# Two attention blocks on one core: fewer bound products, Strassen sums left in PSUM, a different cost for ScalarE in the list scheduler

## The chip, the cores and the metric

The kernel runs on one core of one Trainium2 chip. The core has a matmul engine (TensorE, PE in the profile, with PEld for its weight loads), VectorE (DVE), ScalarE (ACT), GpSimd (POOL), and SyncE (SP), which here only issues DMA transfers. On-chip memory is SBUF; matmul results land in PSUM, which the kernel hands out as eight banks of 128 x 512 float32, and which GpSimd does not touch in this kernel. The metric is the device time of one execution in microseconds. The inputs are float32; for its large products the kernel splits each operand into two float16 halves and multiplies three of the four pairs of halves.

## The reference

Two independent attention blocks over 2048 tokens and 1024 features, 32 heads of 32; their outputs stand side by side.

```python
# block A: causal softmax attention in 4 segments of 512, with a compressive memory
for s in range(4):
    logits = einsum("bhqd,bhkd->bhqk", qs, ks) * scale + mask
    a_dot = softmax(logits) @ vs
    a_mem = (phi(qs) @ M) / (phi(qs) @ z + 1e-6)          # phi(t) = t + 1 if t > 0 else exp(t)
    outs.append(g * a_mem + (1 - g) * a_dot)
    M, z = M + phi(ks).T @ vs, z + sum(phi(ks))
a = concat(outs) @ A_wo
# block B: linear attention with a learned feature map
q, k, v = split(B_x @ B_wqkv)
phi_q = concat(softmax(q @ w_phi), softmax(-(q @ w_phi)))   # phi_k likewise, from k
kv, z = phi_k.T @ v, sum(phi_k)
b = ((phi_q @ kv) / (phi_q @ z + 1e-6)) @ B_wo
out = concat(a, b, axis=-1)
```

## The kernel before

The program runs five stages, one after the other with some overlap. The times are those of the windows in the profile.

1. **Attention of block A** (about 0 to 870 us). There are 32 units: a unit `u` is one segment of 512 tokens and one group of four heads. `produce(u)` projects queries, keys and values of a unit (L369 matmuls into `proj` banks), and `attend(u)` does row maxima (L801, L807), scores (L902), exponentials (L906), the split of the probabilities into halves (L908 on ScalarE, L909 on VectorE), masks (L915 on GpSimd) and the product with the values (L938). Segments 0 and 1 are done for all eight head groups first, then segments 2 and 3. Meanwhile the weights of block B are folded, combined and split in the background (`fold`, `weights_v`, `prepare`).
2. **Values of block B for three of the eight token pairs** (about 870 to 960 us), with `strassen`.
3. **Keys** (about 960 to 1290 us): for each of eight token pairs a Strassen product for keys and, for five pairs, one for values; `expo` makes the two softmaxes of the keys, and L1350 accumulates the key-value sums.
4. **Queries** (about 1290 to 1600 us): Strassen products for queries, `expo` again, the products with the sums, and the output projection of block B (L369 into `misc`).
5. **Output projection of block A** (about 1600 to 1766 us), a Strassen product in place (L1590).

Before a projection is made, its size must be bounded, because the float16 halves need a scale. The bound of a group is the product of the largest column sum of its weights and the largest entry of the segment. `bounds(k, segs)` (queries and keys) and `bounds_v(k, segs)` (values) build it with a tiny matmul that sums over the partitions (L687: 128 x 2, L708: 128 x 1) and a few tiny operations on VectorE and GpSimd. `k` runs over 16 (group, half) pairs for queries and keys and over 8 for values; each call handles two segments with one matmul each.

The weights of a head group are loaded by `load_wg`, scaled and split into float16 halves by `halves`. Its default (`sub=DVE`) is one ScalarE copy with a scale (L396) and one VectorE subtraction (L398); for the first two groups the caller passes `POOL`, which scales and subtracts on GpSimd (L390, L393).

`strassen` makes four 128 x 512 output blocks from seven products of twelve matmuls each. Three PSUM banks X, Y, Z hold the products. Three partial sums are copied from PSUM to SBUF by ScalarE (`keep`, L583), and VectorE adds a product from PSUM to the copy in place (`add`, L587). The callback `out` then reads three of the four blocks from SBUF (tile `cs`, or `pk` in stage 2) and the fourth from the PSUM bank. In stages 3 and 4 `out` is `expo`: two reductions (L1192), two subtractions (L1194, L1196), four exponentials on ScalarE (L1199), a sum (L1202), for keys a multiplication of the 128 x 32 sums by a constant (L1204), and a reciprocal (L1205). For keys GpSimd then multiplies the exponentials by the reciprocals (L1308). For values `out` is `vout` (L1230 on ScalarE, L1232 on VectorE).

The order on each engine is not the order of the Python code. Every operation is recorded with its engine, a cost in microseconds, its reads and writes and a priority; `Graph.run` then places them one by one like a list scheduler: the engine that can start first takes, among its ready operations, the one with the lowest priority number. The costs and the latencies between engines (`Graph.LAT`) are constants in the code. An operation marked `port` on VectorE is not placed while the plan has GpSimd busy, nor the other way round. PSUM banks are given out in the same loop, with a limit for each kind (`MOST`). A DMA issue is an operation on SP; `lanes` are two dummy tiles: loads that write the same lane are placed one behind the other. The real program gets only the resulting order and semaphores for true dependences, so a wrong cost makes no error, only a worse order.

Of the kernel before, what the change touches and what calls it, by code (L numbers as in the profile page):

```python
# [78 lines left out]
class Graph:  # L79
# [35 lines left out]
    def op(self, eng, dur, fn, r=(), w=(), prio=0, lat=0.0, short=False, port=False, need=(), kb=256):  # L115
        o = Op()
        o.short, o.port = short, port or eng == "POOL"
        o.eng, o.dur, o.fn, o.prio, o.lat, o.kb = eng, dur, fn, (prio, len(self.ops)), lat, kb
# [137 lines left out]
def tile_kernel(ctx: ExitStack, tc: tile.TileContext, ax, aw, awv, awo, beta, bx, bwqk, bwv, bphi, bwo, out):  # L256
# [52 lines left out]
    nc.vector.memset(big, 0.0)  # L309
    wsc = const.tile([128, 3, 2, 2], F32, name="wsc")  # L310
# [75 lines left out]
    def halves(hi, lo, src, sc, n, prio, port=True, sub=DVE):  # L386

        (hb, hk, hv), (lb, lk, lv), (sb, sv), (cb, ck, cv) = hi, lo, (src[:-1] if len(src) > 2 else src[0], src[-1]), sc
        if sub == POOL:
# [167 lines left out]
    def xkept(p, slots, prio):  # L557
# [5 lines left out]
        for f in XORDER:  # L563
            b, i = where[f]
            op(SP, 0.6, lambda b=b, i=i, f=f: nc.sync.dma_start(b()[:, i], xf_d[p, :, f]),
               r=[(xfb, (p, f))], w=[(b, (f, a)) for a in range(2)], prio=prio, lat=1.0, kb=256)
        return view_

    def strassen(x, w, prio, kinds, tag, out):
# [16 lines left out]
        def add(t, ps):  # L586
            op(DVE, 0.62, lambda: nc.vector.tensor_tensor(t(), t(), ps(), op=OP.add), r=[ps], w=[t], prio=prio)  # L587
# [4 lines left out]
        add(p1, Y)  # L592
        out(0, 0, p1)
# [5 lines left out]
        add(p5, X)  # L599
        out(1, 1, p5)  # L600
        mult(Z, 5)
        add(u2, Z)
        out(0, 1, u2)
# [21 lines left out]
    pstb, wmb, topb = (G.fixed(t) for t in (pst, wm, tops))  # L625
# [53 lines left out]
    def bounds(k, segs, prio):  # L679


        bd = bds.get(k) or bds.setdefault(k, G.buf("a", [128, 5, 2, 2], F32, "bd", 4))
        s0, n, kk = segs[0], len(segs), k % NG
        v, w = slice(s0 % 2, s0 % 2 + n), [(bd, x % 2) for x in segs]
        ps = bank("misc", [128, 2, 2], "bounds")
        for x in segs:
            op(PE, 0.14, lambda x=x: nc.tensor.matmul(  # L687
                ps()[:, x % 2], xam[:, x:x + 1].to_broadcast([128, 128]), wgb[:, kk], start=True, stop=True),
               r=[(xams, x), (wgbs, (kk, 0)), (wgbs, (kk, 1))], w=[ps], prio=prio, need=[bd])
        op(DVE, 0.1, lambda: nc.vector.tensor_scalar(bd()[:, 3, v], ps()[:, v], 2.0 ** -12, 1e-30, op0=OP.mult, op1=OP.max),  # L690
           r=[ps], w=w, prio=prio)
        op(DVE, 0.12, lambda: nc.vector.reciprocal(bd()[:, 2, v], bd()[:, 3, v]), w=w, prio=prio)
# [778 lines left out]
    for c in range(NT):  # L1471
        P = Q0 + c
        if c % 2 == 0:
# [6 lines left out]
            if c + 2 < NT:  # L1480
                x = xkept(c // 2 + 1, XB if c == 0 else XS, P)
# [180 lines left out]
```

## Time and profile before

| what | us |
|---|---|
| median of 3 runs | 1764.49 (1764.32 to 1765.12) |
| the profiled execution's own time | 1767.9 |
| its span, first to last instruction | 1766.2 |
| PE / DVE / ACT / POOL busy | 1714.1 / 1430.7 / 1147.8 / 978.2 |

The profiled execution lies 3.4 us above the median, and 1.7 us of its time are outside the span. Busy times are unions of the instructions' intervals. A matmul's record runs until its result has drained, so consecutive records overlap, and small waits inside a stream of matmuls do not show as idle time. Groups are listed as "line engine operation out<-in, count | busy us, mean ns of one | idle time before them and what ended it". Tile names are given without their buffer numbers.

### The profile page before, as it was taken

How to read it: one execution, taken by the hardware profiler on the slowest of the kernel's cores; microseconds unless marked ns; L12 is line 12 of the kernel's file. 1: busy time of each engine (PE TensorE's matmuls, PEld its weight loads, DVE VectorE, ACT ScalarE, POOL GpSimd, SP SyncE). 2: the span in 40 equal slices, each digit the busy share in tenths (PEclk: the TensorE clock that was granted, in tenths of full speed). 3: DMA queues.
4: the chain of work that ended last, by engine and by line, in shares of the span. 5: the costliest groups of instructions: out<-in, count | busy, mean ns of one | idle time of the engine just before them, and what ended most of it. 6: DMA issues, size and time to landing. Idle time of an engine off the chain costs nothing.

```text
span 1766.2 us, 39229 instructions
## 1 busy us (share of the span) xinstructions
PE 1714.1 (97%) x14722; PEld 1040.3 (59%) x14722; DVE 1430.7 (81%) x3330; ACT 1147.8 (65%) x2115; POOL 978.2 (55%) x1191
## 2 busy tenths in 40 slices
PE   7999998999999999999999998999999999999999
PEld 5766666767766776776754444544455555554444
DVE  6988998899998887889765999788998888886541
ACT  6878888888787888686863665666444454344431
POOL 6336567654579897756641767545566665430000
PEclk9999999999999999999999999999999999999999
DMA  6545456665665654754556453469213332234311
GB/s 206 178 142 157 133 183 208 199 207 170 215 199 160 182 160 106 228 166 134 172 163 234 168 174 107 144 194 356 102 60 96 109 108 88 63 140 135 120 66 66
DMA packets 194143, 273.64 MB, mean 155 GB/s; under 512 B 72224, under 2 KB 125216, under 8 KB 187424
## 3 DMA queue, kind: packets, MB, share of 16 engines
q1 hardware_dynamic: 193952, 271.13, 48.4%
q8 instruction: 116, 1.90, 0.5%
q14 instruction: 75, 0.61, 0.1%
HBM read 160.12 MB, written 85.00 MB: 139 GB/s over the span
## 4 chain that ended last, share of the span: by engine, by line
PE 52%; DVE 17%; ACT 4%; issue 1%; DMA 1%; POOL 0%; ACTq 0%; DVEq 0%; POOLq 0%
PE proj L369 12%; PE proj L577 11%; PE misc L369 8%; PE proj L1590 5%; PE s L1590 2%; DVE mx L1192 2%; PE s L902 2%; DVE e L1196 2%; PE s L801 2%; PE pv L938 2%; DVE r L1202 2%; DVE e L1194 1%; ACT e L1199 1%; PE misc L1590 1%; PE pv L1536 1%
## 5 line engine op out<-in xcount | busy, mean ns | idle before, releaser
L369 PE MATMUL proj<-S,S 128*128 128x128 f16 (+1 forms) x3072 | 500.9, 299 | 5.6 <-ACT S L396 3.6
L369 PEld LDWEIGHTS <-S 128*128 128x128 f16 x4608 | 331.0, 98 | 154.6 <-issue 9.1
L577 PE MATMUL proj<-S,S 128*128 128x512 f16 x1584 | 368.8, 384 | 11.3 <-DVE cs L587 5.9
L577 PEld LDWEIGHTS <-S 128*128 128x128 f16 x2016 | 193.9, 99 | 234.3 <-issue 20.8
L915 POOL TENSOR_SCALAR_AFFINE_SELECT ph<-ph 128x256 f16<-128x256 f16 (+1 forms) x448 | 194.1, 455 | 158.7 <-DVE ph L909 134.5
L909 DVE SCALAR_TENSOR_TENSOR ph<-s,ph 128x512 f16<-128x512 f32 x320 | 210.1, 683 | 55.6 <-ACT ph L908 53.1
L807 DVE CUSTOM_DVE_ANT_0 s<-s,causal 128x512 f32<-128x512 f32 (+3 forms) x512 | 242.1, 510 | 13.0 <-PE s L801 9.3
L906 ACT ACTIVATE s<-s,bd 128x512 f32<-128x512 f32 x320 | 212.7, 713 | 23.5 <-PE s L902 21.1
L908 ACT ACTIVATE ph<-s 128x512 f16<-128x512 f32 x320 | 191.5, 658 | 0.8 <-PE pv L938 0.2
L369 PE MATMUL misc<-S,ot 128*128 128x512 f16 x768 | 175.3, 381 | 0.0
L1199 ACT ACTIVATE e<-e,sk 128x256 f32<-128x256 f32 x256 | 113.3, 497 | 83.8 <-DVE e L1196 79.2
L369 PEld LDWEIGHTS <-ot 128*128 128x128 f16 x768 | 73.8, 98 | 82.0 <-issue 1.3
L1504 POOL TENSOR_TENSOR e<-e,zb 128x512 f32<-128x512 f32 x64 | 82.0, 1305 | 70.5 <-DVE r L1202 50.0
L902 PE MATMUL s<-S 104*128 104x512 f16 (+3 forms) x512 | 113.0, 299 | 5.5 <-DVE ph L909 3.3
L801 PE MATMUL s<-S 96*128 96x512 f16 (+3 forms) x512 | 113.7, 300 | 2.3 <-DVE ph L909 1.5
L1308 POOL TENSOR_TENSOR e<-e,r 128x1024 f32<-128x1024 f32 x32 | 66.2, 2081 | 76.6 <-DVE r L1205 60.6
L369 PE MATMUL proj<-wv,S 128*128 128x128 f16 x1536 | 103.2, 220 | 0.1
L938 PEld LDWEIGHTS <-ph 128*128 128x128 f16 x2560 | 87.6, 96 | 18.3 <-issue 3.4
L1202 DVE TENSOR_REDUCE r<-e 128x32 f32<-128x1024 f32 x64 | 76.8, 1210 | 25.5 <-ACT e L1199 25.4
L938 PE MATMUL pv<-vl,ph 128*128 128x66 f16 (+1 forms) x2560 | 92.1, 185 | 2.3 <-DVE oall L942 0.9
L1517 POOL TENSOR_TENSOR e<-e,r 128x1024 f32<-128x1024 f32 x32 | 62.3, 1950 | 37.7 <-DVE r L1515 36.4
L807 DVE DVE_READ_ACCUMULATOR2_ANT mt<- 128x1 f32 x512 | 72.3, 141 | 0.0
(305 smaller groups left out, 3369.1 us busy)
## 6 DMA issues: line engine op xcount, KB each, us to landing
S<-xf_d SPq DMA_DIRECT2D x126, 256.0 KB
S<-h SPq DMA_DIRECT2D x192, 128.0 KB
S<-wf_d SPq DMA_DIRECT2D x21, 1024.0 KB
st<-bwqk SPq DMA_DIRECT2D x64, 256.0 KB
out<-os SPq DMA_DIRECT2D x40, 256.0 KB
S<-aw SPq DMA_DIRECT2D x16, 512.0 KB
wa_d<-S SPq DMA_DIRECT2D x16, 512.0 KB
wf_d<-fo SPq DMA_DIRECT2D x32, 256.0 KB
```

What stands on the lines that cost most here:

```text
L369: op(PE, dur, lambda c=c, a=a, b=b, lv=lv, rv=rv: nc.tensor.matmul(pv(), lv(), rv(), start=(c == 0 and a + b == 0), stop=(c == n - 1 and a ...
L577: op(PE, 0.215, lambda n=n, a=a, b=b, lv=lv, rv=rv: nc.tensor.matmul(ps(), lv(), rv(), start=(start and n == 0 and a + b == 0), stop=(n == ...
L801: nc.tensor.matmul(ps()[:, o:o + 128 * i + 128], st()[0:96, 0, h, 128 * i:128 * i + 128], st()[0:96, 1, h, 0:128 * i + 128], start=True, s ...
L807: dve(0.12 + 0.00113 * n, lambda h=h, i=i, o=o, n=n: nc.vector.tensor_tensor_reduce(ps()[:, o:o + n], ps()[:, o:o + n], causal[:, 512 - n: ...
L902: nc.tensor.matmul(ps()[:, o:o + n], st()[0:104, 1, h, 128 * j:128 * j + 128], st()[0:104, 0, h, 128 * j:512], start=True, stop=True)
L906: act(0.59, lambda: nc.scalar.activation(ps(), ps(), AF.Exp, bias=0.0, scale=bd()[:, 4, i2, 0:1]), r=[(bd, i2)], w=[ps])
L908: act(0.5, lambda: nc.scalar.activation(ph()[:, 0], ps(), AF.Copy, scale=2.0 ** 14), r=[ps], w=[(ph, 0)])
L909: dve(0.6, lambda: nc.vector.scalar_tensor_tensor(ph()[:, 1], ps(), 2.0 ** 14, ph()[:, 0], op0=OP.mult, op1=OP.subtract), r=[ps, (ph, 0)], ...
L915: nc.gpsimd.affine_select(pd, pd, pattern=[[0, n], [1, 128]], compare_op=OP.is_ge, fill=0.0, base=0, channel_multiplier=-1)
L938: nc.tensor.matmul(ps()[:, i, n0:n1], ph()[:, a, o:o + 128], vl()[:, j, h, n0:n1], start=(i == 0 and a == 0), stop=(j == min(i, 2)), skip_ ...
L1199: op(ACT, 0.41, lambda i=i: nc.scalar.activation(e()[:, 4 * i:4 * i + 4], e()[:, 4 * i:4 * i + 4], AF.Exp, bias=0.0, scale=sk()[:, i:i + 1 ...
L1590: op(PE, 0.215, lambda n=n, a=a, b=b: nc.tensor.matmul(ps(), v(a)[:, n, :], wform[w]()[:, b, n, :], start=(start and n == 0 and a + b == 0 ...
```

## The change

Six edits, all in one:

- **Bounds.** For `k` of the first half the two small matmuls of a call become one: GpSimd first makes the products (tile `pr`), and one matmul sums them. For the second half (segments 2 and 3) all eight groups, or all four value groups, are handled in one call, and the other seven, or three, calls are gone.
- **Strassen.** `add` writes into the PSUM bank instead of the SBUF copy for two of its three sums, so that `out` reads three of the four blocks from PSUM and one from SBUF. The bank is held until `out` is done.
- **Group weights** of groups 2 to 7 are split with `sub=ACT`: ScalarE scales in place and copies to float16, GpSimd subtracts. VectorE no longer takes part.
- **ScalarE's cost.** In `Graph.op` every ScalarE operation over 0.3 us is charged 0.11 us less, and the 0.11 us is added to the latency of its result.
- **`expo`.** The multiplication of the key sums by a constant goes from VectorE to GpSimd.
- **Loads.** The second token pair of the queries is loaded ahead of the first output weights (`bo`), and both kinds of load are put on the two lanes.

```diff
@@ Graph.op
         o.short, o.port = short, port or eng == "POOL"
+        if eng == ACT and dur > 0.3:
+            dur -= 0.11
+            lat += 0.11
@@ halves
+        if sub == ACT:
+            op(ACT, 0.1 + n * 0.00083, lambda: nc.scalar.activation(sv(), sv(), AF.Copy, scale=cv()[:, 1:2]), r=[(cb, ck)], w=[sb], prio=prio)
+            op(ACT, 0.1 + n * 0.00083, lambda: nc.scalar.activation(hv(), sv(), AF.Copy), r=[sb], w=[(hb, hk)], prio=prio)
+            op(POOL, 0.1 + n * 0.0023, lambda: nc.gpsimd.tensor_tensor(lv(), sv(), hv(), op=OP.subtract),
+               r=[sb, (hb, hk)], w=[(lb, lk)], prio=prio)
+            return
@@ xkept
-               r=[(xfb, (p, f))], w=[(b, (f, a)) for a in range(2)], prio=prio, lat=1.0, kb=256)
+               r=[(xfb, (p, f))], w=[(b, (f, a)) for a in range(2)] + [lanes[f % 2]] * queue, prio=prio, lat=1.0, kb=256)
@@ strassen
-        def add(t, ps):
-            op(DVE, 0.62, lambda: nc.vector.tensor_tensor(t(), t(), ps(), op=OP.add), r=[ps], w=[t], prio=prio)
+        def add(t, ps, o):
+            op(DVE, 0.62, lambda: nc.vector.tensor_tensor(o(), t(), ps(), op=OP.add), r=[t, ps], w=[o], prio=prio)
 
         mult(X, 0, True)
         p1 = keep(X)
         mult(Y, 1, True)
-        add(p1, Y)
-        out(0, 0, p1)
+        add(p1, Y, Y)
+        out(0, 0, Y)
         mult(X, 2)
         u2 = keep(X)
         mult(Z, 3, True)
         p5 = keep(Z)
         mult(X, 4)
-        add(p5, X)
+        add(p5, X, p5)
         out(1, 1, p5)
         mult(Z, 5)
-        add(u2, Z)
-        out(0, 1, u2)
+        add(u2, Z, Z)
+        out(0, 1, Z)
         mult(X, 6)
         out(1, 0, X)
@@ bounds (bounds_v likewise)
+        rest = k >= NG
+        ks = slice(0, NG) if rest else slice(k % NG, k % NG + 1)
+        nk = NG if rest else 1
...
-        for x in segs:
-            op(PE, 0.14, lambda x=x: nc.tensor.matmul(
-                ps()[:, x % 2], xam[:, x:x + 1].to_broadcast([128, 128]), wgb[:, kk], start=True, stop=True),
-               r=[(xams, x), (wgbs, (kk, 0)), (wgbs, (kk, 1))], w=[ps], prio=prio, need=[bd])
+        if n > 1 and not rest:
+            pr = G.buf("a", [128, 2, nk, 2], F32, "pr", 1)
+            op(POOL, 0.2, lambda: nc.gpsimd.tensor_tensor(
+                pr(), xam[:, s0:s0 + n, None, None].to_broadcast(shape), wgb[:, None, ks].to_broadcast(shape), op=OP.mult),
+               r=[(xams, x) for x in segs] + wg, w=[pr], prio=prio)
+            op(PE, 0.14, lambda: nc.tensor.matmul(ps(), one.to_broadcast([128, 128]), pr(), start=True, stop=True),
+               r=[pr], w=[ps], prio=prio, need=[bd])
+        else:
+            for x in segs:
+                op(PE, 0.14, lambda x=x: nc.tensor.matmul(
+                    ps()[:, x % 2], xam[:, x:x + 1].to_broadcast([128, 128]), wgb[:, ks], start=True, stop=True),
+                   r=[(xams, x)] + wg, w=[ps], prio=prio, need=[bd])
@@ the loop over units
-            x = 2 * ((u // 4 + 1) // 4)
-            bounds_v(u // 4 + 1, [x, x + 1], 2 * u + 0.5)
+            if u // 4 + 1 <= 4:
+                x = 2 * ((u // 4 + 1) // 4)
+                bounds_v(u // 4 + 1, [x, x + 1], 2 * u + 0.5)
...
-            load_wg(k + 2, 2 * u + 3.5)
-            x = 2 * ((k + 2) // NG)
-            bounds(k + 2, [x, x + 1], 2 * u + 3.5)
+            load_wg(k + 2, 2 * u + 3.5, ACT)
+            if k + 2 <= NG:
+                x = 2 * ((k + 2) // NG)
+                bounds(k + 2, [x, x + 1], 2 * u + 3.5)
@@ expo
-            op(DVE, 0.1, lambda: nc.vector.tensor_scalar(r(), r(), 1.0 / up, None, op0=OP.mult), r=[r], w=[r], prio=prio)
+            op(POOL, 0.15, lambda: nc.gpsimd.tensor_scalar(r(), r(), 1.0 / up, None, op0=OP.mult), r=[r], w=[r], prio=prio)
@@ ahead of the queries
+    x, x1 = xkept(0, XS, PB + 12.9), xkept(1, XB, P + 2, True)
     bo = [[G.buf("slot", [128, 2, 4, 512], F16, f"S{4 + 2 * n + q}") for q in range(2)] for n in range(2)]
...
-               w=[(bo[n][q], (a, i)) for a in range(2) for i in range(4)], prio=P + 1, lat=1.0, kb=1024)
+               w=[lanes[q]] + [(bo[n][q], (a, i)) for a in range(2) for i in range(4)], prio=P + 1, lat=1.0, kb=1024)
```

Line numbers of the changed kernel are larger (L369 becomes L373, L577 becomes L587, L587 becomes L597, L1192 to L1205 become L1242 to L1255). What the scheduler makes of it is shown at three places.

VectorE in the key stage, at the sums and the softmaxes of one Strassen product, before (`cs` is the SBUF copy; `e`, `mx` and `r` are exponents, extrema and sums):

```order
L587 TENSOR_TENSOR cs<-cs,s 128x512
L1205 RECIPROCAL r<-r 128x32
L378 TENSOR_REDUCE ast<-ast 128x1
L1194 TENSOR_TENSOR e<-cs,mx 128x16x32
L1196 TENSOR_TENSOR e<-mx,cs 128x16x32
L1192 TENSOR_REDUCE mx<-cs 128x16 x2
L1202 TENSOR_REDUCE r<-e 128x32
L1204 TENSOR_SCALAR r<-r 128x32
L1205 RECIPROCAL r<-r 128x32
L587 TENSOR_TENSOR cs<-cs,misc 128x512
```

and VectorE in the key stage after the change:

```order
L597 TENSOR_TENSOR misc<-cs,misc 128x512
L1432 RECIPROCAL osc_109<-osc_109 128x1
L1242 TENSOR_REDUCE mx<-misc 128x16 x2
L1244 TENSOR_TENSOR e<-misc,mx 128x16x32
L1246 TENSOR_TENSOR e<-mx,misc 128x16x32
L1282 SCALAR_TENSOR_TENSOR ot<-cs,pst,ot 128x8x64
L1252 TENSOR_REDUCE r<-e 128x32
L1255 RECIPROCAL r<-r 128x32 x2
L597 TENSOR_TENSOR cs<-cs,proj 128x512
```

The sum is written to the bank (`misc<-cs,misc`), the four operations behind it read the bank, and the multiplication between the sum of the exponentials and the reciprocal is no longer there.

GpSimd in the key stage, before:

```order
L1308 TENSOR_TENSOR e<-e,r 128x1024
L1343 TENSOR_TENSOR pt<-e,pt 128x512
L1308 TENSOR_TENSOR e<-e,r 128x1024 x2
L1109 TENSOR_TENSOR zb<-zb 128x512
L1308 TENSOR_TENSOR e<-e,r 128x1024
```

and after:

```order
L1254 TENSOR_SCALAR r<-r 128x32
L1358 TENSOR_TENSOR e<-e,r 128x1024
L1393 TENSOR_TENSOR pt<-e,pt 128x512
L1254 TENSOR_SCALAR r<-r 128x32
L1358 TENSOR_TENSOR e<-e,r 128x1024
L1225 TENSOR_SCALAR sk<-swf,pst 128x4
L1254 TENSOR_SCALAR r<-r 128x32 x2
L1358 TENSOR_TENSOR e<-e,r 128x1024 x2
```

The small multiplication stands in GpSimd's queue right ahead of the large one that needs the reciprocal made from it.

ScalarE in the attention stage while the weights of one head group are split, before (the `S` tiles with `wgs` are the weights):

```order
L396 ACTIVATE S_3865<-S_3760,wgs 128x512
L829 ACTIVATE S_149<-misc 8x512
L906 ACTIVATE s<-s,bd 128x512 x2
L908 ACTIVATE ph<-s 128x512 x2
L906 ACTIVATE s<-s,bd 128x512 x2
L908 ACTIVATE ph<-s 128x512 x2
```

and after:

```order
L394 ACTIVATE S_3962<-S_3962,wgs 128x512 x2
L814 ACTIVATE z<-proj,bd 128x512
L888 ACTIVATE vl_120<-vf_125,bv 128x16x32
L395 ACTIVATE S_4204<-S_3962 128x512
L1166 ACTIVATE fp<-S_3139 128x512
L641 ACTIVATE pkt<-misc 128x512
L395 ACTIVATE S_4204<-S_3962 128x512
L394 ACTIVATE S_3962<-S_3962,wgs 128x512
```

Each quarter of the weights takes two ScalarE operations (L394 and L395) instead of one, and they are mixed with the unit's other copies.

101 lines of the change are left out of this document (64 added, 37 removed).

## The prediction

> **What bounds the kernel.** I read the page's first part and its chain, then busy times by stage, then who PE waits for.
>
> ```profile
> span 1766.2 us, 39229 instructions
> PE 1714.1 (97%) x14722; PEld 1040.3 (59%) x14722; DVE 1430.7 (81%) x3330; ACT 1147.8 (65%) x2115; POOL 978.2 (55%) x1191
> ...
> PE 52%; DVE 17%; ACT 4%; issue 1%; DMA 1%; POOL 0%; ACTq 0%; DVEq 0%; POOLq 0%
> ```
>
> PE is busy for 1714.1 of 1766.2 us, so only 52 us of the span are idle time on PE. The chain runs over VectorE for 17%, mostly while PE has other work. What a lighter VectorE is worth must therefore be looked for in PE's idle time, stage by stage (columns: PE, PEld, DVE, ACT, POOL busy, clock, DMA share, GB/s):
>
> ```profile
> 30.00:400.00 370.00, 357.21 (x3805) 253.66 (x3804) 326.23 (x930) 308.40 (x559) 220.17 (x333) 0.99 0.58 178
> 400.00:900.00 500.00, 499.08 (x5474) 352.81 (x5472) 429.78 (x1245) 392.91 (x713) 358.74 (x537) 1.00 0.58 171
> 900.00:1600.00 700.00, 675.06 (x4570) 344.86 (x4570) 588.16 (x1007) 367.81 (x730) 382.72 (x295) 0.99 0.43 145
> 188.00:229.00 41.00, 39.26 (x487) 29.18 (x485) 37.10 (x105) 40.90 (x73) 27.26 (x46) 1.00 0.42 138
> 247.00:285.00 38.00, 33.82 (x396) 24.79 (x394) 29.46 (x73) 37.79 (x70) 29.56 (x45) 0.91 0.48 132
> ```
>
> Attention idles PE for 12.8 us in its first part and for 0.9 us in its second; keys and queries (900 to 1600) for 24.9 us. The last two rows are stretches of the first part in which ScalarE is busy without a gap (40.9 of 41 us, 37.8 of 38 us): there VectorE has room and ScalarE sets the pace; in the second PE idles 4.2 us and its granted clock is 0.91. PE's waits from 900 to 1600:
>
> ```profile
> PE proj L577 <- DVE cs L587: 5.9, 4, 4.2
> PE kv L1350 <- DVE pt L1343: 5.5, 7, 1.6
> PE proj L577 <- ACT cs L583: 5.3, 3, 2.8
> ```
>
> These are waits for the sums and copies of the Strassen products and for the split of the keys, two of three on VectorE.
>
> **Fewer bound products.**
>
> The groups (count, busy us, mean ns), and from the chain in order of time one bank's twelve matmuls in the last stage (start, us):
>
> ```profile
> L687 PE MATMUL misc<-wgb,xam 128*128 128x2 f32 x64 | 9.2, 240 | 0.0
> L708 PE MATMUL misc<-wvb,xam 128*128 128x1 f32 x32 | 4.7, 243 | 0.0
> ...
> L1590 PE MATMUL misc<-S,ot 128*128 128x512 f16 x96 | 22.0, 379 | 0.0
> ...
> L699 POOL TENSOR_SCALAR bd<-bd 128x4 f32<-128x4 f32 x14 | 3.1, 220 | 0.0
> ```
>
> ```profile
> 1619.65 2.59 PE misc L1590 x12
> ```
>
> Two records are one float32 matmul, so 48 matmuls stand here, and 19 remain: 10 in the old form and 9 single ones on a product made by GpSimd. The 29 that go cost 13.9 us / 48 = 0.29 us each in busy time, 8.4 us. Part of a record is drain that lies under the next matmul: twelve matmuls of 0.379 us take 2.59 us, 0.216 each, so 0.163 us of each is covered. With that, a bound matmul costs 0.29 - 0.163 = 0.127 us and 29 of them 3.7 us. Ends 3.7 and 8.4; I take 5 us off PE, since short float32 records stand between other matmuls but load new weights. The added GpSimd products are nine, at L699's 0.22 us some 2 us, and off the path: bounds are made three units (of 870 / 32 = 27 us) ahead of their use.
>
> **Strassen sums in PSUM, and the moved multiplication.**
>
> ```profile
> L1194 DVE TENSOR_TENSOR e<-cs,mx 128x512 f32<-128x512 f32 x48 | 40.2, 838 | 0.0
> L1194 DVE TENSOR_TENSOR e<-proj,mx 128x512 f32<-128x512 f32 x16 | 10.8, 676 | 0.0
> L1196 DVE TENSOR_TENSOR e<-mx,cs 128x512 f32<-128x512 f32 x48 | 49.6, 1034 | 0.0
> L1196 DVE TENSOR_TENSOR e<-mx,proj 128x512 f32<-128x512 f32 x16 | 10.8, 675 | 0.0
> L1204 DVE TENSOR_SCALAR r<-r 128x32 f32<-128x32 f32 x32 | 11.9, 375 | 0.2
> L1232 DVE SCALAR_TENSOR_TENSOR ot<-cs,pst,ot 128x512 f16<-128x512 f32 x15 | 20.2, 1357 | 0.0
> L1232 DVE SCALAR_TENSOR_TENSOR ot<-proj,pst,ot 128x512 f16<-128x512 f32 x5 | 3.7, 734 | 3.6 <-ACT ot L1230 3.6
> L587 DVE TENSOR_TENSOR cs<-cs,proj 128x512 f32<-128x512 f32 x39 | 26.7, 684 | 28.7 <-PE proj L577 25.5 <-ACT cs L583 1.9 <-DMA S<-xf_d 1.2
> ```
>
> The same operation is shorter when its source is a bank. Two of three `cs` readers move: 32 x (0.838 - 0.676) = 5.2 us, 32 x (1.034 - 0.675) = 11.5 us, 10 x (1.357 - 0.734) = 6.2 us, and 11.9 us of L1204 leave: 34.8 us of VectorE's 588 in this stage. The plan charges these readers 0.6 us whatever the source, so the order also gets nearer to the truth. A sum written to a bank is in no row; by the shortest and longest rows above (0.675 and 1.034 us) 48 sums would move by -0.4 to +17 us of VectorE. I take no change, since these already read a bank at 0.684. What reaches the end is bounded by PE's idle time: at most 24.9 us; at least 0, if PE's waits are set by order, not load; below 0 if the held banks delay PE (a rival). Of the three waits above, 11.4 of 16.7 us are on VectorE, and its load falls by 6%: I take half of the idle time, 12 us. The moved multiplication puts GpSimd into the path between L1202 and L1205:
>
> ```profile
> L1308 POOL TENSOR_TENSOR e<-e,r 128x1024 f32<-128x1024 f32 x32 | 66.2, 2081 | 76.6 <-DVE r L1205 60.6 <-DVE r L1204 15.8
> ```
>
> GpSimd waits 76.6 us for these reciprocals already, and the small operation (about 0.22 us) stands right ahead of its consumer; behind a late one wait GpSimd's key splits and VectorE's reciprocal. At worst a reciprocal waits for one 2.08 us operation; I cost it nothing, since five exponent buffers rotate, and 12 us above would shrink if that cover fails.
>
> **Group weights.**
>
> ```profile
> L398 DVE SCALAR_TENSOR_TENSOR S<-S,wgs,S 128x512 f16<-128x512 f32 x24 | 20.0, 858 | 0.6 <-ACT S L396 0.6
> L396 ACT ACTIVATE S<-S,wgs 128x512 f16<-128x512 f32 x24 | 17.0, 759 | 2.8 <-DVE wgs L384 2.7
> L392 ACT ACTIVATE S<-S 128x512 f16<-128x512 f32 x8 | 5.0, 624 | 5.9 <-POOL S L390 5.8
> L393 POOL TENSOR_TENSOR S<-S,S 128x512 f16<-128x512 f32 x8 | 9.7, 1234 | 0.9 <-ACT S L392 0.9
> ```
>
> and from the timeline (start, us):
>
> ```profile
> 599.41 0.64 ACT L908 ACTIVATE ph<-s 128x512 f16<-128x512 f32 x1
> 599.89 0.72 ACT L906 ACTIVATE s<-s,bd 128x512 f32<-128x512 f32 x1
> 600.46 0.69 ACT L475 ACTIVATE fp<-S 128x512 f16<-128x512 f32 x1
> ```
>
> VectorE loses 24 operations, 20 us, in the first 330 us. GpSimd gets 24 x 1.23 = 30 us on 220 of 370: hidden, the weights are loaded three units ahead. ScalarE keeps a scaled copy and gets 24 plain ones. A copy of 0.624 us occupies ScalarE for about 0.1 less when another follows (above, 0.64 starts 0.48 ahead of the next): 24 x 0.52 = 12.5 us more. VectorE's relief is worth at most the 12.8 us of idle; but the longest of it lies where ScalarE is packed, so I take 3. ScalarE's 12.5 us cost between 0 and 12.5; packed stretches are 79 of 370 us, a fifth, so I take 3.
>
> **ScalarE's cost in the plan.** The three timeline rows show starts 0.48 and 0.57 us apart. The plan of before charges 0.50 (L908) and 0.59 (L906): that is already the distance between starts. Minus 0.11 it plans 0.39 and 0.48, 0.09 us too little each; the latency put back keeps a lone result's time right, but in the 73 operations of the 41 us stretch the plan would run 6.6 us ahead of the chip. ScalarE then lags, and PE, in order, waits for scores whose probabilities aren't ready; behind it wait the projections that would have filled the gap. Upper end: 32 units x 20 score operations x 0.09 = 58 us. Lower end: 0, or some gain by luck of the order. PE idles 0.9 us in the 500 us where the costs were true, so this is mostly downside; yet on average ScalarE has a fifth of its time free there (392.9 of 500), in which it catches up. I take 5.
>
> The Trainium skill, "ScalarE: Activation LUTs", section "What ACT_TABLE_LOAD costs", states that ScalarE operations issued back to back overlap by about 93 ns; the rows above agree (0.64 us long, 0.48 apart is more). By that rule alone, for a table of full durations, this edit would repair the plan, and the sum would be 5 us better. The rows say that the table holds no full durations.
>
> **Queued loads.** The next pair's form of the tokens now stands on SP ahead of the output weights, and the first projection of block B waits for those; Strassen products can fill in. PE's waits from 900 to 1600 name no DMA, so I put 0, with one of the waits above, 5.9 us, as the end on either side.
>
> **Sum.** -5 -12 -3 +3 +5 = -12 us. The profiled execution took 1767.9 us (1.7 outside its span), so the next one would be about 1756; the median lies 3.4 us lower than the profiled one, at 1764.5, so I forecast 1752. Its own range is 1744 to 1761, from 20 and 3 us for VectorE's relief.
>
> **Rivals.**
> - *Nothing but the bounds moves.* PE at 97% hides VectorE anyway; then 1764.5 - 5 = 1759.5. Against it: VectorE is in two of three waits.
> - *All idle goes.* -5 - 24.9 - 10 of attention's 12.8: 1724.6. Against it: packed ScalarE, and in-order waits always leave some.
> - *ScalarE lags its plan.* If PE waits for half of the 58 us, +29 in place of +5: 1776.5. It decides above 17 us (the other four terms), 0.027 us per score operation, a third of the undercount. For it: two fully packed stretches, and the clean second half of attention. This one ends slower.
> - *Held banks.* A bank stays taken for four more reads of 0.675 us, 2.7 us, and the second and third bank of 24 Strassen products are such. If PE waits for half of one each, 24 x 1.35 = 32 us, and VectorE's 12 stay: 1764.5 - 12 + 32 = 1784.5. Against it: X, which `out` also reads from its bank before, is the last one free, and the next product starts with X.
>
> **Chances.** Forecast 0.38, bounds only 0.14, all idle 0.10, ScalarE's lag 0.28, held banks 0.10. About 0.2% (3.5 us, 1761 to 1768) is what a measurement tells from no change. Faster: 0.37 of the forecast, 0.08 of bounds only, 0.10, and 0.02 of the two slower rivals at their mild ends, 0.57. Same: 0.01 + 0.06 + 0.04 = 0.11. Slower 0.32. From 1728 to 1784 about 0.07 is left out below and 0.13 above.
>
> **What would show it.** Right: L687 and L708's successors together 38 records; subtractions from banks near 0.68 us; `r` scaled on GpSimd; VectorE's busy time near 1376 us (34.8 and 20 less); PE's idle time from 900 to 1600 at half. Wrong: PE idle of more than some us between 400 and 900 with releasers L954 to L957 (the scores' exponentials and splits), or `proj`, `misc` or `s` matmuls waiting for `e` or `mx`.

## The result and the profile after

The changed kernel takes 1791.75 us (median of 4 runs, 1789.62 to 1793.40) against 1764.8 us for the kernel before on the same chip: 1.0145 of its time, 95% interval 1.0122 to 1.0168. It is slower by some 26 us where 12 us less was forecast, and lies 8 us above the range.

The first part of the page, of the changed kernel, with the chain's shares:

```profile
span 1787.9 us, 39129 instructions
PE 1716.0 (96%) x14664; PEld 1033.4 (58%) x14664; DVE 1367.0 (76%) x3245; ACT 1160.6 (65%) x2139; POOL 998.7 (56%) x1232
...
PE 29%; DVE 12%; ACT 3%; issue 1%; POOL 1%; DMA 0%; DVEq 0%; ACTq 0%; POOLq 0%
```

VectorE is busy for 1367.0 us, 64 less than before, and PE for about as long as before; the span is 21.7 us longer, and PE's idle time grows by 19.8 us. By stage (columns: PE, PEld, DVE, ACT, POOL busy, clock, DMA share, GB/s), changed kernel:

```profile
30.00:400.00 370.00, 347.47 (x3661) 242.75 (x3660) 302.16 (x877) 314.53 (x568) 237.35 (x358) 1.00 0.54 167
400.00:900.00 500.00, 477.04 (x5144) 334.49 (x5144) 402.14 (x1179) 374.06 (x680) 342.04 (x482) 1.00 0.56 164
900.00:1600.00 700.00, 686.18 (x4814) 354.33 (x4813) 554.85 (x1005) 382.57 (x759) 391.49 (x360) 1.00 0.45 150
```

PE idles 22.5 us in attention's first part (12.8 before), 23.0 in its second (0.9 before) and 13.8 in keys and queries (24.9 before). So one half of the change gained where it should, and attention lost more. In attention's second part ScalarE isn't overloaded: it is busy for 374.1 us, less than the 392.9 before. PE's longest waits of attention (30 to 925 us), changed kernel (total, times, longest, in us):

```profile
PE s L849 <- DVE ph L957: 6.8, 15, 1.0
PE misc L875 <- DVE mh L870: 4.0, 3, 1.7
PE pv L986 <- DVE ph L957: 3.3, 7, 0.9
PE misc L922 <- ACT pkt L641: 3.2, 5, 1.1
PE s L950 <- DVE ph L957: 3.1, 7, 0.8
```

The same view of the kernel before has, for L957's old line:

```profile
PE s L902 <- DVE ph L909: 3.3, 4, 1.5
PE s L801 <- DVE ph L909: 1.5, 1, 1.5
PE pv L938 <- DVE ph L909: 0.9, 1, 0.9
```

In these rows PE waits 13.2 us instead of 5.7 for the low half of the probabilities, which VectorE makes from ScalarE's high half, and in 29 short stalls instead of 6. VectorE's own longest wait over the span is for that high half; the kernel before, then the changed one:

```profile
DVE ph L909 <- ACT ph L908: 53.1, 69, 3.4
```

```profile
DVE ph L957 <- ACT ph L956: 113.9, 134, 5.0
```

And ScalarE's timeline in the changed kernel (start, duration, us), where it is packed:

```profile
601.08 0.77 ACT L954 ACTIVATE s<-s,os 128x512 f32<-128x512 f32 x1
601.65 0.80 ACT L814 ACTIVATE pq<-proj,os 128x512 f32<-128x512 f32 x1
602.22 0.78 ACT L954 ACTIVATE s<-s,os 128x512 f32<-128x512 f32 x1
```

The starts are 0.57 us apart, as before. The plan now charges L954, one of the two score operations, 0.48. (The windows are at fixed times, and attention ends some 30 us later here than before, so the third row holds a little more of it.)

### The profile page after: what moved, and what is told of

Its sections match the earlier page's. It is cut to its first block, busy times and chain, and to the rows that moved or that the text cites. A ratio compares the mean times of both kernels' runs of the same rounds, so it can differ in the third digit from the quotient of the medians.

```text
span 1787.9 us, 39129 instructions
## 1 busy us (share of the span) xinstructions
PE 1716.0 (96%) x14664; PEld 1033.4 (58%) x14664; DVE 1367.0 (76%) x3245; ACT 1160.6 (65%) x2139; POOL 998.7 (56%) x1232
## 5 line engine op out<-in xcount | busy, mean ns | idle before, releaser
L373 PE MATMUL proj<-S,S 128*128 128x128 f16 (+1 forms) x3072 | 500.5, 300 | 4.8 <-ACT S L406 3.2
L373 PEld LDWEIGHTS <-S 128*128 128x128 f16 x4608 | 328.8, 98 | 158.7 <-issue 17.9
L587 PE MATMUL proj<-S,S 128*128 128x512 f16 x1584 | 361.5, 379 | 1.6 <-ACT cs L593 1.3
L587 PEld LDWEIGHTS <-S 128*128 128x128 f16 x2016 | 192.5, 98 | 221.4 <-issue 4.7
L957 DVE SCALAR_TENSOR_TENSOR ph<-s,ph 128x512 f16<-128x512 f32 x320 | 212.5, 686 | 116.0 <-ACT ph L956 113.9
L855 DVE CUSTOM_DVE_ANT_0 s<-s,causal 128x256 f32<-128x256 f32 (+3 forms) x512 | 242.4, 509 | 6.4 <-PE s L849 3.2
L373 PE MATMUL misc<-S,ot 128*128 128x512 f16 x768 | 173.7, 379 | 0.0
L1249 ACT ACTIVATE e<-e,sk 128x256 f32<-128x256 f32 x256 | 113.9, 498 | 65.3 <-DVE e L1246 64.8
L373 PEld LDWEIGHTS <-ot 128*128 128x128 f16 x768 | 73.4, 98 | 82.2
L954 ACT ACTIVATE s<-s,os 128x512 f32<-128x512 f32 x160 | 110.8, 740 | 13.0 <-PE s L950 9.3
L954 ACT ACTIVATE s<-s,bd 128x512 f32<-128x512 f32 x160 | 106.3, 700 | 5.9 <-PE s L950 3.6
L373 PE MATMUL proj<-wv,S 128*128 128x128 f16 x1536 | 104.1, 219 | 0.6 <-DVE mt L855 0.5
L1567 POOL TENSOR_TENSOR e<-e,r 128x1024 f32<-128x1024 f32 x32 | 61.8, 1936 | 28.4 <-DVE r L1565 19.6
```

Source lines behind the costliest of these rows:

```text
L373: op(PE, dur, lambda c=c, a=a, b=b, lv=lv, rv=rv: nc.tensor.matmul(pv(), lv(), rv(), start=(c == 0 and a + b == 0), stop=(c == n - 1 and a ...
L587: op(PE, 0.215, lambda n=n, a=a, b=b, lv=lv, rv=rv: nc.tensor.matmul(ps(), lv(), rv(), start=(start and n == 0 and a + b == 0), stop=(n == ...
L855: dve(0.12 + 0.00113 * n, lambda h=h, i=i, o=o, n=n: nc.vector.tensor_tensor_reduce(ps()[:, o:o + n], ps()[:, o:o + n], causal[:, 512 - n: ...
L954: act(0.59, lambda: nc.scalar.activation(ps(), ps(), AF.Exp, bias=0.0, scale=bdv()[:, 3, i2, 0:1]), r=[(bd, i2)], w=[ps])
L957: dve(0.6, lambda: nc.vector.scalar_tensor_tensor(ph()[:, 1], ps(), 2.0 ** 14, ph()[:, 0], op0=OP.mult, op1=OP.subtract), r=[ps, (ph, 0)], ...
L1249: op(ACT, 0.41, lambda i=i: nc.scalar.activation(e()[:, 4 * i:4 * i + 4], e()[:, 4 * i:4 * i + 4], AF.Exp, bias=0.0, scale=sk()[:, i:i + 1 ...
```

## Experiments

Every ratio is to the kernel before on the same chip, with its 95% interval.

**The cost taken out, and put in alone.** First, the changed kernel without the edit of ScalarE's cost:

```diff
-        if eng == ACT and dur > 0.3:
-            dur -= 0.11
-            lat += 0.11
```

> The changed kernel with ScalarE's costs as before; the other five edits stay. Theory A (the 0.11 us taken off ScalarE's costs makes the plan run ahead of ScalarE): the time falls under that of the kernel before, to 1742-1756, and PE idles less than 3 us between 400 and 900 us. Theory B (the group weights on ScalarE and GpSimd, in stretches where ScalarE is packed): the time stays at 1780-1792 and the idle time of PE stays at 10 us or more between 30 and 400. Theory C (any new order loses the luck of the old one): 1765-1790, with idle time spread as in the changed kernel.

Second, these three lines as the only edit of the kernel before:

> The kernel before with the cost edit alone. Theory A: the whole loss and more, 1785-1805, PE idle of 15 us or more between 400 and 900, waits of PE for VectorE's split of the probabilities (L909) behind a late ScalarE copy. Theory B: no change, 1762-1768. Theory C: some loss, 1770-1790, and a cost change a tenth of its size loses as much.

Measured: without the edit 1750.8 us, 0.9907 [0.9893, 0.9922]; the edit alone 1817.11 us, 1.0281 [1.0265, 1.0296]. Attention's second part, first without it, then it alone:

```profile
400.00:900.00 500.00, 491.26 (x5352) 344.44 (x5351) 421.59 (x1204) 385.06 (x703) 351.47 (x509) 1.00 0.58 168
```

```profile
400.00:900.00 500.00, 480.94 (x5207) 339.93 (x5206) 421.32 (x1186) 375.82 (x679) 346.89 (x508) 0.99 0.56 164
```

The edit costs 50 us alone (0.0281 x 1764.5) and 42 among the others (1.0145 less 0.9907 is 0.0238). Alone it idles PE 19.1 us in this stretch against 0.9, and VectorE waits for the high halves:

```profile
DVE ph L912 <- ACT ph L911: 82.2, 114, 4.7
```

That is between the 53.1 us of before and the 113.9 of the change. So the loss is this edit's, and the change without it is faster. Two figures miss what was expected: the edit alone costs more than the 1785 to 1805 us named, and without it PE still idles 8.7 us from 400 to 900 us, not under 3.

**Is it the undercount, or only another order?** The planner can make a new order from any new number. The same lines with smaller numbers, with the latency alone, and with ScalarE charged too much:

```diff
+            dur -= 0.01     # second kernel: 0.055; third: not there; fourth: += 0.05
+            lat += 0.01     # second kernel: 0.055; third: 0.11;      fourth: -= 0.05
```

> The kernel before with 0.01 us instead of 0.11 us moved from ScalarE's cost to its latency: a new order at nearly true costs. Theory A: within 4 us of the kernel before, 1761-1769, since the costs are true to 0.03 us either way. Theory C: 1770-1790, as any new order.

> The kernel before with half of the cost edit (0.055 us). Theory A, the loss grows with the undercount (about 0.035 us per operation instead of 0.09): 1775-1797, between the tenth (1772) and the whole (1817). Theory C, any new order costs about the same: 1768-1776.

> The kernel before with 0.11 us added to the latency of ScalarE's results and nothing taken off their cost. Theory A (the undercount of ScalarE's occupancy is the loss): no loss like the whole edit's 49 us; 1762-1778, at most the price of a new order (5 us for the tenth) or some us more. If the latency is what hurts: 1790 or more.

> The kernel before with ScalarE charged 0.05 us too much in place of too little. If a cost that is too low is what hurts: 1760-1775, at most the price of a new order. If any wrong cost hurts as much: 1778 or more, as the half edit in the other direction (1784.7).

Measured:

| edit of the kernel before | us | ratio | PE idle, 400 to 900 us | PE waits for ScalarE, 30 to 925 us (times) |
|---|---|---|---|---|
| none | 1764 to 1770 | 1 | 0.9 | 1.0 (2) |
| 0.01 less, latency 0.01 more | 1772.28 | 1.0028 [1.0017, 1.0039] | 10.5 | 3.1 (7) |
| 0.055 less, latency 0.055 more | 1784.71 | 1.0092 [1.0073, 1.0111] | 6.2 | 6.5 (13) |
| 0.11 less, latency 0.11 more | 1817.11 | 1.0281 [1.0265, 1.0296] | 19.1 | 14.2 (18) |
| latency 0.11 more alone | 1770.08 | 1.0008 [0.9999, 1.0018] | 10.0 | 2.9 (6) |
| 0.05 more, latency 0.05 less | 1772.08 | 1.0022 [1.0008, 1.0035] | 7.9 | 0.7 (1) |

The idle times are 500 less PE's busy time in one row of each kernel, as here for 0.01 less, then for the latency alone:

```profile
400.00:900.00 500.00, 489.50 (x5280) 344.39 (x5279) 424.07 (x1234) 376.40 (x682) 345.60 (x512) 0.99 0.56 166
```

```profile
400.00:900.00 500.00, 490.01 (x5266) 346.13 (x5264) 419.44 (x1213) 375.91 (x684) 345.73 (x511) 0.98 0.57 166
```

The last column adds up the rows of the view of PE's waits that name ScalarE itself. The largest are, for the whole edit alone,

```profile
PE s L804 <- ACT pk L769: 3.9, 5, 1.3
PE misc L877 <- ACT pkt L634: 2.8, 3, 1.6
PE s L804 <- ACT oT L634: 2.5, 4, 1.0
```

and for the kernel before

```profile
PE misc L1043 <- ACT oT L631: 0.6, 1, 0.6
```

Two things are apart here. Every kernel of this document whose attention has another order of matmuls idles PE 5 us or more in the almost gapless stretch of the kernel before: 0.01 us, too little to matter as a cost, brings 10.5 us of idle time there, and 5 us at the end. The idle time of this one stretch doesn't rank the kernels (half of the edit has 6.2 us). On top of the new order comes the undercount. Against the starts in the timeline, 0.48 and 0.57 us apart, the plan of 0.01 less still charges the two score operations enough (0.49 and 0.58), 0.055 less charges them 0.035 too little, and 0.11 less 0.09 too little: 5, 16 and 50 us. The loss rises with the undercount; three orders are too few to say whether faster than in proportion. The latency alone changes the time by 0.08%, within the interval of no change, so the loss needs the shorter occupation (that without the added latency wasn't run). Charging too much costs no more than a new order does.

PE's waits for ScalarE itself rise with the undercount too; in the changed kernel they are 12.1 us in 20 waits, and without the edit 2.3 us in 5. Its waits for the low half of the probabilities don't sort the kernels: over all rows they are 6.1 us before, 10.4 with the latency alone, which loses nothing, and 8.4 with the whole edit alone, which loses 50. Nor does VectorE's wait for the high half: 50.7 us in 86 waits with half of the edit, less than before. So PE's waits for ScalarE's results of all kinds go with the loss; the low half of the probabilities is only a part of it.

**Where on ScalarE?** The same undercount on the two score operations only, and no others:

```diff
-            act(0.59, ... AF.Exp ...)
+            act(0.48, ... AF.Exp ..., lat=0.11)
-            act(0.5, ... AF.Copy, scale=2.0 ** 14 ...)
+            act(0.39, ... AF.Copy, scale=2.0 ** 14 ..., lat=0.11)
```

> The kernel before with the cost edit on the two score operations alone (the exponential and the split's copy, 640 of some 1,960 operations that the edit touches). Theory A with the price that I gave, 32 units x 20 score operations: most of the 49 us, 1795-1815, nearly all of it in the attention stage. If all of ScalarE's operations count alike: a third of it, 1775-1788.

Measured: 1798.71 us, 1.0174 [1.0159, 1.0189]: 31 of the 50 us, 62%. VectorE's wait for the high halves is here

```profile
DVE ph L909 <- ACT ph L908: 69.6, 113, 2.7
```

with 113 waits for 69 before. The scores carry most of it, and the other ScalarE operations, 38% by this difference, aren't nothing; with some 5 us between one order and another, the two shares are rough.

**The group weights.** The kernel before with the new split of the weights as its only edit; the changed kernel without it (the cost edit stays); and the changed kernel with neither:

```diff
-            load_wg(k + 2, 2 * u + 3.5, ACT)
+            load_wg(k + 2, 2 * u + 3.5)
```

> The kernel before with the group weights of groups 2 to 7 split by ScalarE and GpSimd, nothing else. By my sum: VectorE's relief 3 us against ScalarE's extra work 3 us, 1762-1768. Theory B: 1775-1790 with the loss between 30 and 400 us, where 12.5 us of ScalarE's time are added. Theory A says nothing of it beyond the sum.

> The changed kernel with the group weights split as before; the cost edit stays. Theory A: the cost edit is the loss, 1780-1795, as the changed kernel. Theory B: below 1772, since ScalarE's packed stretches are relieved.

> The changed kernel with ScalarE's costs as before and the group weights split as before (ScalarE and VectorE); bounds, Strassen sums, moved multiplication and queued loads stay. If the group weights cost by themselves what they cost alone on the kernel before (21 us): 1725-1738. If that loss was the luck of an order: 1745-1758, within some us of the run without the cost edit.

Measured: the split alone 1788.71 us, 1.0125 [1.0108, 1.0142]; the change without it 1803.37, 1.0194 [1.0173, 1.0215]; with neither 1733.14, 0.9800 [0.9784, 0.9816], the fastest of all kernels here, and faster than both. Beside the true costs the split thus costs 0.9907 less 0.9800, 1.1% or 19 us; beside the false ones taking it out made things worse (1.0194 against 1.0145). One stretch of the changed kernel without the split, with the cost edit, shows how:

```profile
400.00:450.00 50.00, 37.52 (x285) 24.32 (x284) 43.47 (x126) 34.85 (x66) 21.10 (x37) 0.80 0.53 159
```

```profile
PE pv L986 <- POOL ph L963: 4.2, 1, 4.2
PE misc L1018 <- POOL osum L1013: 3.2, 1, 3.2
```

PE idles 12.5 of 50 us, partly in single waits of 4.2 and 3.2 us for GpSimd, and the granted clock falls to 0.80. An order made with false costs can go wrong in one place, whatever edit set it off, so this run doesn't tell what the split is worth.

The split alone lands in the range of theory B, but not by its reason: from 30 to 400 us, which holds nearly all of the 24 splits, PE idles 10.1 us, less than the 12.8 before. It idles more afterwards, 8.5 for 0.9 us from 400 to 900 and 26.6 for 20.3 from 900 to 1300. That speaks for a worse order in this kernel, and against the added operations themselves.

The fastest kernel (neither edit), then the one with the split added and true costs, from 30 to 400 and 400 to 900 us:

```profile
30.00:400.00 370.00, 363.88 (x3887) 258.02 (x3885) 332.60 (x952) 318.04 (x574) 226.72 (x351) 1.00 0.60 182
400.00:900.00 500.00, 495.00 (x5397) 348.02 (x5396) 423.55 (x1232) 391.13 (x713) 352.18 (x510) 1.00 0.58 172
```

```profile
30.00:400.00 370.00, 358.52 (x3837) 255.63 (x3836) 315.11 (x918) 324.21 (x590) 246.69 (x370) 0.99 0.59 178
400.00:900.00 500.00, 491.26 (x5352) 344.44 (x5351) 421.59 (x1204) 385.06 (x703) 351.47 (x509) 1.00 0.58 168
```

In the first stretch VectorE is relieved of 17.5 us, and PE idles 5.4 us more; in the second 3.7 more. Half of the 19 us is seen as PE's idle time here. Which engine is it? The split without the cost edit, once with GpSimd scaling and subtracting (ScalarE then only copies), once with ScalarE scaling and VectorE subtracting:

```diff
-            load_wg(k + 2, 2 * u + 3.5, ACT)
+            load_wg(k + 2, 2 * u + 3.5, POOL)
```

```diff
-            op(POOL, 0.1 + n * 0.0023, lambda: nc.gpsimd.tensor_tensor(lv(), sv(), hv(), op=OP.subtract), ...)
+            op(DVE, 0.07 + n * 0.00104, lambda: nc.vector.tensor_tensor(lv(), sv(), hv(), op=OP.subtract), ..., port=True)
```

> The changed kernel without the cost edit (1750.8) and with the group weights scaled by GpSimd too, so that ScalarE has one copy for each as in the kernel before and GpSimd two operations, VectorE none. If ScalarE's added 24 scalings are what the group weights cost: back to 1731-1742. If the cost is the longer way over GpSimd (weights late, their raw tile held longer): 1750 or more.

> The changed kernel without the cost edit (1750.8), with the subtraction of the group weights on VectorE: ScalarE still has the 24 added scalings, GpSimd nothing of the weights. If GpSimd's 24 subtractions are what costs: 1731-1741, near the run with the weights as before (1733.1). If the cost is ScalarE's, or that the scaled copy stands in the raw tile: 1745-1756.

Measured: GpSimd scaling and subtracting 1749.65 us, 0.9897 [0.9882, 0.9911]; VectorE subtracting 1744.21 us, 0.9864 [0.9846, 0.9882]. So more work on ScalarE isn't needed for the loss. One suspicion was left: the new scaled copy may itself be charged too little. In the changed kernel's timeline two of them (L394) take from 78.03 to the next start at 79.25, 0.61 us each, and its charge is 0.1 + 512 x 0.00083 = 0.525 before the edit of the cost:

```profile
78.03 1.47 ACT L394 ACTIVATE S<-S,wgs 128x512 f32<-128x512 f32 x2
79.25 1.28 ACT L395 ACTIVATE S<-S 128x512 f16<-128x512 f32 x2
```

The charge was raised, once with GpSimd and once with VectorE subtracting:

```diff
-            op(ACT, 0.1 + n * 0.00083, lambda: nc.scalar.activation(sv(), sv(), AF.Copy, scale=cv()[:, 1:2]), ...)
+            op(ACT, 0.19 + n * 0.00083, lambda: nc.scalar.activation(sv(), sv(), AF.Copy, scale=cv()[:, 1:2]), ...)
```

> The changed kernel without the cost edit, in which the scaled copy of the group weights is charged 0.19 + 512 x 0.00083 = 0.615 us, the distance between its starts in the trace, in place of 0.525. If the loss from the group weights (0.9907 against 0.9800) is an undercount of its own, 24 x 0.09 us, then most of it comes back: a ratio of 0.980 to 0.985. If it is the extra work and steps themselves, the ratio stays between 0.989 and 0.992.

> The same charge of 0.615 us, and VectorE subtracts in place of GpSimd (0.9864 with the charge of 0.525). If the undercount is the cause of what is left there, 0.980 to 0.982; if ScalarE's additional copies are, 0.985 to 0.988.

Measured: 1762.01 us, 0.9967 [0.9956, 0.9977], worse by 0.6% than with the false charge, and 1744.73 us, 0.9866 [0.9852, 0.9879], the same as with it. The suspicion falls: 24 operations undercharged by 0.09 us aren't the cause. In all five variants of the changed kernel with a new split and without the cost edit the time is longer than without the split: by 11 and 12 us with VectorE subtracting, by 17, 19 and 29 with GpSimd. That GpSimd's subtraction is part of the loss agrees with all five, but the figures with GpSimd differ among themselves by up to 12 us, more than the 5 us that separate the nearest of the two groups (a single charge moved one of them by 0.6%). What makes up the remaining 11 us, the extra ScalarE copies or the loss of a good order, these runs do not settle.

**The parts of the gain.** Two edits alone on the kernel before, the Strassen sums and the bounds; and from the fastest kernel two taken back, the multiplication of the key sums on VectorE again and the loads as before:

```diff
-            op(POOL, 0.15, lambda: nc.gpsimd.tensor_scalar(r(), r(), 1.0 / up, ...))
+            op(DVE, 0.1, lambda: nc.vector.tensor_scalar(r(), r(), 1.0 / up, ...))
```

```diff
-    x, x1 = xkept(0, XS, PB + 12.9), xkept(1, XB, P + 2, True)
-               w=[lanes[q]] + [(bo[n][q], (a, i)) ...], prio=P + 1, lat=1.0, kb=1024)
+               w=[(bo[n][q], (a, i)) ...], prio=P + 1, lat=1.0, kb=1024)
+    x = xkept(0, XS, PB + 12.9)
-                x = x1 if c == 0 else xkept(c // 2 + 1, XS, P)
+                x = xkept(c // 2 + 1, XB if c == 0 else XS, P)
```

> The kernel before with the Strassen sums in PSUM alone. By my sum: 22.9 us less of VectorE and some 8 us less idle time of PE between 900 and 1600, so 1755-1762 if the attention stage keeps its order; the held-banks rival: 1770-1790, with matmuls into proj, misc or s waiting for the softmax of the bank.

> The kernel before with the bounds edit alone. My sum has -5 us of PE (3.7 to 8.4) and nothing else: 1757-1763 if the order stays as good. The run without cost edit and group weights gained 18 us in the attention stage, where this is the only edit left: if it is the bounds' work on VectorE, GpSimd and the bank, 1745-1755.

> The best run (1733.1: changed kernel without cost edit and group weights) with the multiplication of the key sums back on VectorE. If that move is the missing gain of 19 us: 1745-1755, with more idle time of PE in the key stage. If not: 1730-1739.

> The best run (1733.1) with the loads at the start of the queries as before. If the queued loads are the missing gain: 1745-1755, with idle time of PE where keys end and queries begin. If not: 1730-1739.

Measured: Strassen sums 1759.09 us, 0.9948 [0.9932, 0.9965]; bounds 1761.73, 0.9963 [0.9950, 0.9976]; multiplication back 1745.0, 0.9871 [0.9853, 0.9888], so that moving it is worth 0.9871 less 0.9800, 0.7% or 12.5 us; loads back 1740.65, 0.9848 [0.9831, 0.9865], so that they are worth 0.5% or 8.5 us. The four add up to 0.52 + 0.37 + 0.71 + 0.48 = 2.08%, and together they measured 2.00%. The loads' 1740.65 us lies between the two ranges named for it. The key stage, first of the kernel with the multiplication back on VectorE, then of the fastest:

```profile
900.00:1300.00 400.00, 381.76 (x2644) 193.26 (x2643) 335.84 (x580) 230.94 (x469) 216.94 (x175) 1.00 0.51 173
```

```profile
900.00:1300.00 400.00, 390.44 (x2696) 199.71 (x2694) 320.37 (x561) 234.22 (x478) 229.48 (x210) 0.99 0.52 176
```

PE idles 18.2 us with it on VectorE and 9.6 with it on GpSimd. With the loads as before the same stretch has 14.2, and PE's longest wait from 900 to 1600 us isn't for a DMA:

```profile
PE kv L1397 <- ACT pt L1387: 4.4, 1, 4.4
```

PE's waits there name no transfer at all. That the loads act through the order which the planner makes around them is the reading left, and it wasn't tested by itself.

## Why the prediction was wrong

Step by step, each against what was measured for it (shares of 1764.5 us):

| step | predicted, us | measured, us |
|---|---|---|
| fewer bound products | -5 (-3.7 to -8.4) | -6.5 |
| Strassen sums | -12 with the multiplication (0 to -24.9) | -9.2 |
| moved multiplication | within that 12 | -12.5 |
| queued loads | 0 (-5.9 to 5.9) | -8.5 |
| group weights | -3 + 3 = 0 | 19 without the cost edit |
| ScalarE's cost in the plan | 5 (0 to 58) | 42 to 50 |
| sum | -12 | 26 |

The first two rows were measured as the only edit, the next three beside other edits, and the last both ways, so that they need not add up to 26 exactly.

- **ScalarE's cost: the step that failed.** "... in which it catches up. I take 5." The mechanism was in the prediction (the table holds distances between starts; minus 0.11 it plans 0.09 too little; ScalarE lags, PE waits in order), and so was an upper end of 58 us. What failed is the argument that an engine with a fifth of its time free catches up. ScalarE was even less busy there than before (374.1 of 500 us, in part because the whole stage ran slower), and PE still idled 23.0 us. Free time on average didn't help. The reading is that the order puts each matmul right behind the planned end of the ScalarE work that it needs, and the work that could fill the gap stands behind the waiting matmul. By the row of the kernel before, 0.9 us of idle in 500, the order had nothing to spare, and the prediction itself called the edit mostly downside. It should have taken the upper half of its range: the score operations alone took 31 of their 58 us, and all of ScalarE's operations 50. PE's waits for ScalarE itself, 1.0 us before, 6.5 with half of the edit and 14.2 with the whole, agree with it; that fill work stood behind the waiting matmuls was not tested apart from the undercount.
- **The rival "ScalarE lags its plan"** is what happened. Its price, half of 58, was too low, and with 0.28 it stood behind a forecast whose only support against it was the mean load. It was said to decide above 17 us, or 0.027 us per operation; 0.055 us less charged, 0.035 too little for a score operation by the timeline, cost 16 us, of the 22 us that 640 such operations add up to.
- The Trainium skill, "ScalarE: Activation LUTs", section "What ACT_TABLE_LOAD costs", states that operations issued back to back overlap by about 93 ns. The rows that the prediction shows give more, 0.15 to 0.16 us (0.72 and 0.64 us long, 0.57 and 0.48 apart). By that rule alone, for a table of full durations, the sum would have been 5 us better; the run with only this edit took 50 us more. The overlap is real, but the old charges of the two score operations contained it already.
- **Group weights, mis-sized at 0.** "I take 3" for VectorE's relief and 3 for ScalarE. No gain from VectorE's relief shows: 17.5 us less on VectorE from 30 to 400 us came with 5.4 us more of PE idle. GpSimd's 24 subtractions were costed at nothing ("hidden, the weights are loaded three units ahead"); with VectorE doing them the loss was 11 to 12 us instead of 17 to 29. Which part failed, the added operations or the order that they led to, stays open. (ScalarE's part was also read loosely: the row shows a copy of 0.64 us that starts 0.48 ahead of the next, 0.16 less and not 0.1, so that 24 of them are 11 us and not 12.5.)
- **Strassen sums and the multiplication: right in kind, too small.** Idle time from 900 to 1600 fell from 24.9 to 13.8 us, by about half as predicted. But the two edits, each measured by itself, add up to 21.7 us, not 12. PE's idle time was the wrong measure of what there was to gain. In the fastest kernel

```profile
PE 1696.6 (98%) x14664; PEld 1032.1 (60%) x14664; DVE 1377.0 (80%) x3269; ACT 1146.9 (66%) x2115; POOL 976.0 (56%) x1208
```

  PE's busy time is 17.5 us shorter than before, of which the bounds took 9.7 when they were the only edit (1714.1 - 1704.4), and its idle time is another 17.5 us shorter (1731.2 - 1696.6 = 34.6, from 52.1). So about half of the gain stood in PE's busy column. The multiplication on GpSimd, which the prediction put within the same 12 us, was worth 12.5 us, against 9.2 for the sums. (GpSimd's 76.6 us of waiting, in the prediction "for these reciprocals", are 60.6 for the reciprocals and 15.8 for the multiplication ahead of them.) The sums into a bank cost nothing extra, as taken: they lie at

```profile
L597 DVE TENSOR_TENSOR cs<-cs,proj 128x512 f32<-128x512 f32 x21 | 14.3, 679 | 13.2 <-PE proj L587 11.7 <-DMA S<-xf_d 1.2 <-ACT cs L593 0.3
...
L597 DVE TENSOR_TENSOR proj<-cs,proj 128x512 f32<-128x512 f32 x18 | 12.4, 691 | 29.0 <-PE proj L587 29.0
```

  0.691 us into the bank and 0.679 into the copy.
- **Held banks** were not seen: in the changed kernel PE's waits from 900 to 1600 name no VectorE reader of a held bank (L1242 to L1246). GpSimd's `e` (L1567, 1.6 us) is an operand in SBUF. The longest is

```profile
PE kv L1400 <- DVE pt L1393: 2.6, 4, 1.1
```

- **Bounds: right.** The records in the profile after are 38, as said (12 + 8 + 6 + 4 + 4 + 4), and -6.5 us lies between the ends. With the bounds alone PE's busy time fell by 9.7 us, more than the 8.4 taken as the upper end, of which 6.5 reached the end. The records:

```profile
L709 PE MATMUL misc<-pr,one 128*128 128x4 f32 x12 | 2.1, 248 | 0.5 <-DVE ph L957 0.3 <-ACT oT L641 0.2
L713 PE MATMUL misc<-wgb,xam 128*128 128x2 f32 x8 | 1.3, 247 | 0.0
L747 PE MATMUL misc<-pr,one 128*128 128x2 f32 x6 | 1.0, 232 | 0.0
...
L751 PE MATMUL misc<-wvb,xam 128*128 128x4 f32 x4 | 0.6, 211 | 0.0
```

- **Queued loads: missed.** The waits named no DMA, from which 0 was read. By the reading above, a load's place in the order also moves what the planner puts around it, which no view of the trace before shows.
- Of the marks named beforehand, VectorE at 1376 us (1367.0 measured), the bounds' records, the bank subtractions (0.675 us from `proj`, below) and idle time at half came out; so did the sign that it was wrong, PE idle between 400 and 900 with waits for L957.

```profile
L1244 DVE TENSOR_TENSOR e<-proj,mx 128x512 f32<-128x512 f32 x34 | 23.0, 675 | 0.0
```

## What to carry to other kernels

A planner's cost for an engine is the distance between starts, and it must not be below the distance that the chip shows: read that distance off the timeline for each form of operation before a constant is subtracted from all of them. When PE executes a fixed order with almost no gap, an undercount on another engine doesn't average out against that engine's free time; price it as undercount times operations, and treat "it catches up" as a claim to be shown. And when several edits share one planner, test each alone and without the others: here four of six gave 2.0% together, and two took 3.5% away.

## What was not expected of the hardware and the order

A change of 0.01 us in the planned costs moved the time by 0.28% [0.17, 0.39], and a truer charge for 24 operations moved it by 0.6% the wrong way (0.9967 from 0.9907). The kernel before had a stretch of 500 us with 0.9 us of PE idle, which none of the five orders with other ScalarE costs in the table above reached again. So the single parts, of 0.4 to 0.7%, are each no larger than what one order differs from another by; that the four of them add up to 2.08% against 2.00% measured speaks for them together, not for each to the tenth.

The traces narrow this for three of the four. With the Strassen sums alone, PE's first 9,400 matmul records, until 905 us, follow one another as in the kernel before by tile names and sizes, and the gapless stretch stays (498.46 of 500 us busy). The kernels with the multiplication and the loads taken back share their first 9,737 and 11,434 records with the fastest, until 957 and 1201 us. So no other order of matmuls in attention stands behind what these three edits gain, though the order after it differs.

The move of the small multiplication, 32 operations of some 0.3 us on either engine, was worth 12.5 us, about as much as all of its 11.9 us on VectorE:

```profile
L1254 POOL TENSOR_SCALAR r<-r 128x32 f32<-128x32 f32 x32 | 9.9, 315 | 62.7 <-DVE r L1252 62.4 <-DVE tops L507 0.2
```

GpSimd takes 0.315 us for one, against VectorE's mean of 0.375 before.
